# Weights converted into the tiles that TensorE reads, and sums of two batches on VectorE, in a fused attention and mixer kernel

## The chip, the cores and the metric

The kernel runs on one core of a Trainium2 chip. Five engines take part: TensorE (PE; PEld is its loading of weights), VectorE (DVE), ScalarE (ACT), GpSimd (POOL) and SyncE (SP), which here issues every transfer. The metric is the device time of one execution in microseconds, as the median of several runs.

## The reference, cut to what matters

Attention over 4 batches, 12 heads, 448 tokens and 64 channels a head, with a capped score, then two mixers on the result x (4 x 448 x 768):

```python
s = scale * q @ k.T
s = cap * tanh(s / cap)
attn = exp(s - max) / (sum(exp(s - max)) + 1e-9);  x = attn @ v

theta = x @ w_theta                          # 768 x 768
y = w_tok_r @ (x * cos(theta)) + w_tok_i @ (x * sin(theta))   # over tokens
u = x + y;  x = u + relu(u @ w_ch)           # 768 x 768

h = relu(x.T @ w_tok1) @ w_tok2              # 448 -> 256 -> 448, over tokens
u = x + h.T
out = u + relu(u @ w_ch1) @ w_ch2            # 768 -> 1536 -> 768
```

q, k and v come as 32-bit floats, the weights of the mixers as 64-bit floats. The kernel therefore has to turn every weight from a 64-bit word into two 32-bit halves, a high part rounded to the format that TensorE multiplies fast (f32r), and the low rest.

## The kernel before

**Batches.** Attention runs over all four batches, two heads (a head pair) at a time, in four steps of keys for each pair: 24 pairs, 96 steps. The mixers run over two batches at a time: first pair (batches 0 and 1), then second pair (2 and 3). In the first pair the token part (theta and the products over tokens) is done for batch 0 and batch 1 apart, woven into the remaining attention; the second pair follows with no attention left.

**Products.** Every mixer product is three passes, high x high, high x low, low x high (`mm3`), each pass a 128x128 weight tile against 128x448. `gemm(ui, i, ps)` does 18 such passes for one unit of 128 output channels. A unit is a `w` tile of two halves of 768 columns. 36 units make the stream: 0 to 5 w_theta, 6 to 11 w_ch, then four of w_ch1 and four of w_ch2 in turn, three times. `stream` reads w_theta twice in the first pair (batch 0, batch 1), so it has 6 + 36 + 36 places.

**Conversion.** `conv` takes the next piece of the list `conv_list` (half a unit, 128x384, or a part of a token weight): `fetch` loads the 64-bit words into a `raw` tile, and `convert` makes the value with two scalings (`cw` and `raw`; which engine is in `CV` by phase), a shift and an or on VectorE, an add on GpSimd, and then the high half by a cast and the low half by a difference. Before, both halves are written into a small tile `ch`, stored into a cache in HBM (`cu` for units, `ct` for the token weights), and `unit` or `tokmix_gen` loads them again into `w` or `WT`, in the first pair as in the second. One unit is loaded ahead (`AHEAD` = 1); three `w` tiles exist.

**Attention step.** `scores` has TensorE write scores into a bank (`sp`), ScalarE take tanh and exp into a tile `t` (`tm` for the short first step). `av` multiplies with v three steps later (`LAG`). The exponentials' sums come partly from TensorE (products with ones) and partly by adding tiles `t` to one another first: `SUMS` says on which engine, for batches 0 and 1, and 2 and 3 ('p' GpSimd, 'v' VectorE, 'n' none). `finish` copies product and sums out (`EVC`: 'a' ScalarE, 'v' VectorE), sends the sums through HBM to make their inverse (`pk`, `sr`) and broadcast it back (`dn`), and multiplies (`xr` or `XT` with `dn`). The result is split into the halves `XHL`; batches 2 and 3 are put aside in HBM (`xd`) and fetched again (`xl`).

**Token part.** `theta(m)` makes one unit of theta, reduces it to a fraction of a turn on VectorE (`rc`) and takes two sines on ScalarE, which needs another function table than tanh and exp. `zt` transposes the products (`tp`) and splits them into `zn`, `mix` multiplies with the token weights (`tm<-WT,zn` in the trace, a name shared with the short attention tile). `SEQ` gives the order of these steps (t theta, z transposes, x mix, u split, w token weights).

**Order.** Everything is first recorded with a priority by its place in the program. A planner then sets the order on every engine: an engine takes the ready operation of lowest number, and buffers of a ring (`SB`, `PS`) go out in the order in which the program asks for them. `weave` mixes two streams by a ratio (`RATIO`), `every` lets a number of conversions run after each attention step (`PAT`, `PAT1`, `PAT2`), `pri` shifts priorities. Lines of all operations are one helper's line in the trace (L397), so that tiles are read by name.

Of the kernel before, what the change touches and what calls it, by code (L numbers as in the profile page):

```python
# [14 lines left out]
F32R = mybir.dt.float32r  # L15
# [5 lines left out]
B, H, S, D = 4, 12, 448, 64  # L21
DM = H * D
# [13 lines left out]
TWOPI = 6.283185  # L36
HALFPI = float(math.pi / 2)
CW = 384
EVC = 'av'
LAG = 3  # L40
AHEAD = 1
SB = {'kq': 2, 'vt': 2, 'hl': 1, 't': 3, 'tm': 2, 'sv': 2, 'dn': 1, 'xr': 2, 'pk': 3, 'rq': 2, 'w': 3, 'raw': 3, 'cw': 2, 'ch': 2, 'wg': 4, 'zx': 5, 'rc': 4}
PS = {'pa': 2, 'pm': 4}
SUMS = ('pn', 'pp')
CV = ('vvav', 'aavv', 'aaav')
QK = ('vp', 'vp')
XSP = ('v', 'p', 'v')
ZM = ("vv", "pp")
SEQ = ('t0 t1 t2 t3 w z0 x0 t4 z1 x1 t5 u01 z2 x2 z3 x3 u23 z4 x4 u4 z5 x5 u5', 't0 w t1 z0 x0 t2 z1 x1 t3 z2 x2 t4 z3 x3 t5 z4 x4 u01234 z5 x5 u5')
SEQR = "w00 w01 w10 w11 w20 w21 T00 w30 w31 T01 n00 w40 w41 T10 n01 w50 w51 s00 s01 T11 n10 T20 n11 s10 s11 T21 n20 n21 s20 s21"  # L50
CORD = ((0, 0), (1, 0), (0, 1), (2, 0), (1, 1), (3, 0), (2, 1), (3, 1))
CLOSE = 1
ACCM = 2
QREC = 'v'
NATIVE = 2
# [3 lines left out]
PUSH = 15.0  # L59
FIRST = 38  # L60
SECOND = 24
RATIO = ((55, 80.0), (400.0, 130.0))
PAT = (1, 0)
PAT1 = (1, 0, 0)
PAT2 = (1, 0, 0, 0)


def regroup(shape, pattern, sizes):
# [344 lines left out]
def attn_mix_kernel(ctx: ExitStack, tc: tile.TileContext, kqd, vd, cap, wu, wtok, wt1, wt2, out):  # L413
# [5 lines left out]
    pp = ctx.enter_context(tc.tile_pool(name="pp", bufs=1, space=bass.MemoryType.PSUM))  # L419

    plan = Plan(nc)
    plan.tags = {**SB, **PS}
    pe, act, dve, pool, sp_ = (Engine(plan, e) for e in ("PE", "ACT", "DVE", "POOL", "SP"))
    uid = [0]

    def sbuf(name, tag, free, dt=F32, **k):
        uid[0] += 1
        n = f"{name}_{uid[0]}"
        return plan.buf(lambda: sb.tile([P, *free], dt, name=n, tag=tag, bufs=SB[tag]), tag, free, **k)

# [4 lines left out]
    def dram(name, rows, free, whole=False):  # L435
        ap = pd.tile([rows, *free], F32, name=name)
        b = plan.buf(lambda: ap, None if whole else "dram", free, parts=rows, cells=(lambda x: x * 0) if whole else None)
        return b
# [24 lines left out]
    @contextmanager  # L463
    def pri(off):
        plan.off += off
        yield
        plan.off -= off

    def f(v):
        return v.bitcast(F32)  # L470
# [4 lines left out]
    def hi(dst, src):  # L475
        act.copy(dst, src)
# [7 lines left out]
    def times(e, dst, src, by):  # L484
        if e == "a":
            act.mul(dst, src, by)
        else:
            dve.tensor_scalar(out=dst, in0=src, scalar1=by, scalar2=None, op0=ALU.mult)
# [20 lines left out]
    with pri(30):  # L509
# [7 lines left out]
        for j in range(2):  # L517
            at = pick[:, j:j + 1]
# [21 lines left out]
    def fetch(key, src, rows, n):  # L540
        raw = sbuf("raw", "raw", [CW, 2], U32, cells=lambda x: x % 2)[:rows, :n]
        sp_.dma_start(raw.rearrange("p n two -> p (n two)"), src.bitcast(U32))
        return key, raw, rows, n

    def convert(key, raw, rows, n):
        lw, hw = raw[:, :, 0], raw[:, :, 1]
        scale, low, high, rest_ = CV[phase[0]]
        wv = sbuf("cw", "cw", [CW], U32)[:rows, :n]
        times(scale, f(wv), f(hw), 2.0**-112)
        times(low, lw, lw, 2.0**-29)  # L550
        dve.tensor_scalar(out=wv, in0=wv, scalar1=3, scalar2=None, op0=ALU.logical_shift_left)
        dve.scalar_tensor_tensor(out=wv, in0=hw, scalar=0x80000000, in1=wv, op0=ALU.bitwise_and, op1=ALU.bitwise_or)
        pool.tensor_tensor(out=wv, in0=wv, in1=lw, op=ALU.add)
        wv = f(wv)
        hl = sbuf("ch", "ch", [2, CW], F32R)[:rows, :, :n]
        if high == "a":
            hi(hl[:, 0], wv)
        else:
            dve.tensor_copy(out=hl[:, 0], in_=wv)
        (lo_pool if rest_ == "p" else lo)(hl[:, 1], wv, hl[:, 0])  # L560
        name, i, j = key
        if (name, i) not in cache:
            cols = {"u": DM, "t": S, "a": 4 * DT, "b": 2 * S}[name]
            cache[name, i] = dram(f"c{name}{i}", rows, [2, cols])
        sp_.dma_start(cache[name, i][:, :, j * n:(j + 1) * n], f(hl))
# [26 lines left out]
    fetched = []  # L592
    done = set()

    def conv(n=1):
        for _ in range(n):
            while len(fetched) < 3:
                p = next(pieces, None)
                if p is None:
                    break  # L600
                with pri(-60):
                    fetched.append(fetch(*p))
            if fetched:
                x = fetched.pop(0)
                convert(*x)
                done.add(x[0])

    def weight(name, i, dst, parts):
        while any((name, i, j) not in done for j in range(parts)):
            conv()  # L610
        if dst is not None:
            sp_.dma_start(f(dst), cache[name, i])

    WT = {}
    WS = {}

    def tokmix_gen(pr):
        for i in range(4):
            n = min(2, NT7 - 2 * i)
            t = sbuf("WT", "wg", [2, 2 * S], F32R)  # L620
            for j in range(n):
                weight("t", 2 * i + j, t[:, :, j * S:(j + 1) * S], 2)
                WT[2 * i + j] = t[:, :, j * S:(j + 1) * S]
                yield

    def load_tok(pr):
        w1 = [sbuf("W1", "rc", [1024], F32R)[:CP] for h in range(2)]
        w2 = [sbuf("W2", "rc", [1024], F32R)[:, :2 * S] for h in range(2)]
        for name, w, parts in (("a", w1, NK), ("b", w2, 4)):
            weight(name, 0, None, parts)  # L630
            for h in range(2):
                sp_.dma_start(f(w[h]), cache[name, 0][:, h])
        WS[1] = [w.rearrange("p (c o) -> p c o", o=DT) for w in w1]
        WS[2] = [w.rearrange("p (c o) -> p c o", o=S) for w in w2]

    stream = order[:6] + order + order
    units = {}

    def unit(i):
        for j in range(i, min(i + AHEAD + 1, len(stream))):  # L640
            if j not in units:
                t = sbuf("w", "w", [2, DM], F32R)
                with pri(-100):
                    weight("u", stream[j], t, DM // CW)
                units[j] = t
        return units[i]
# [5 lines left out]
    def attn(batches):  # L652
# [45 lines left out]
        def av(b, hp, c):  # L698
            vt, hl, kq, acc, pt = st[b, hp]
            mode = SUMS[b // 2]  # L700
            if c == 0:
                if b < ACCM:
                    acc = [psum("av"), None]
# [60 lines left out]
        def finish(b, hp, acc):  # L764
            if b < CLOSE:
                return close(b, hp, acc)
# [39 lines left out]

    EV = EVC

    def split(dst, src):
# [4 lines left out]
        hi(h, src)  # L814
        (lo_pool if XSP[phase[0]] == "p" else lo)(l, src, h)

# [14 lines left out]
    def token(pr, which):  # L831
# [64 lines left out]

        for op in SEQ[pr].split():
            k, m = op[0], op[1:]
# [25 lines left out]
    def rest(pr):  # L924
# [12 lines left out]
        def tok1(t, i):  # L937
            W1 = WS[1]
            xn = [sbuf("xn", "zx", [1024], F32R)[:CP] for h in range(2)]
# [21 lines left out]
        def tok2(t, i):  # L961
            h1, W2 = h1s[t, i], WS[2]
            for j in range(2):
# [73 lines left out]
    def run(gen):  # L1037
        for _ in gen:
            pass
# [6 lines left out]
    ga = attn(range(B))  # L1046
    run(every(steps(ga, FIRST), PAT))
    phase[0] = 1
    weave(token(0, (0,)), every(steps(ga, SECOND), PAT1), *RATIO[0])
    weave(chain(token(0, (1,)), rest(0)), every(ga, PAT2), *RATIO[1])  # L1050
    late[0] = True
# [46 lines left out]
```

## Time and profile before

| | |
|---|---|
| median of 3 runs | 975.23 us (974.08 to 976.71) |
| profiled execution | 978.4 us, its span 976.6 us |
| granted TensorE clock, mean | 0.993 |
| TensorE, VectorE, ScalarE, GpSimd busy | 956.8, 540.5, 413.6, 270.8 us |
| moved by transfers | 173.62 MB, mean 178 GB/s |

The span goes from the first to the last instruction; what the profiled execution takes beyond it lies before and behind. Times in the trace are counted from the start of the span. Matmuls are pipelined: the time of one (367 ns for 448 columns) is its passage, and what counts for the sum is the distance from start to start. An entry in brackets behind an instruction is the idle time of its engine ahead of it, and who ended it. The granted clock is a share of the full 2.4 GHz.

### The profile page before, as it was taken

Reading aid. Unit: us, or ns where it says so; the run is one execution under the profiler, and the core shown is the slowest. Engines: PE = TensorE matmul, PEld = TensorE weight load, DVE = VectorE, ACT = ScalarE, POOL = GpSimd, SP = SyncE. Lnnn points to the kernel's source line nnn. Section 1 sums busy time; section 2 is a strip of 40 time slices with the busy share of each in tenths; the row PEclk is TensorE's granted clock in tenths of the full one; section 3 lists DMA queues with packets and bytes.
Section 4 is the critical chain, followed back from the end, with each engine's and each line's share of the span. In section 5 each row is a group of like instructions: output and inputs, shape, how many; then the busy total and the mean of one; then the engine's idle time right before and its main releaser. Section 6 shows DMA issues by size and latency. Waiting matters only on the chain.

```text
span 976.6 us, 13210 instructions
## 1 busy us (share of the span) xinstructions
PE 956.8 (98%) x4938; PEld 733.5 (75%) x4938; DVE 540.5 (55%) x927; ACT 413.6 (42%) x645; POOL 270.8 (28%) x208
## 2 busy tenths in 40 slices
PE   9999999999999999999999999999999999999998
PEld 2223445476778886877877799899999889999997
DVE  7776577779876679774656672243623441212222
ACT  7788887748762546433443340333401221010010
POOL 3544234654532455441422340313200000000000
PEclk9999989999999999999999999999999999999999
DMA  7866867558567665796686678611311203223233
GB/s 246 272 199 190 259 199 240 164 166 280 184 182 254 214 218 186 234 313 209 209 271 205 217 249 301 253 37 61 108 65 65 65 1 130 97 97 130 81 132 127
DMA packets 76488, 173.62 MB, mean 178 GB/s; under 512 B 9864, under 2 KB 52744, under 8 KB 76424
## 3 DMA queue, kind: packets, MB, share of 16 engines
q1 hardware_dynamic: 76424, 172.78, 54.3%
q8 instruction: 39, 0.64, 0.3%
q14 instruction: 25, 0.20, 0.1%
HBM read 130.94 MB, written 41.68 MB: 177 GB/s over the span
## 4 chain that ended last, share of the span: by engine, by line
PE 84%; DVE 6%; DMA 5%; ACT 3%; issue 2%; POOL 0%; SPq 0%; ACTq 0%; DVEq 0%; POOLq 0%
PE c L397 36%; PE wc L397 9%; PE av L397 7%; PE tm L397 7%; PE th L397 7%; PE sp L397 7%; PE t L397 5%; DMA dn<-sr 4%; PE sm L397 3%; PE xp L397 2%; DVE rc L397 2%; DVE ch L397 1%; PE tp L397 1%; ACT t L397 1%; DVE cw L397 1%
## 5 line engine op out<-in xcount | busy, mean ns | idle before, releaser
L397 PE MATMUL c<-g,w 128*128 128x448 f32 x864 | 179.1, 367 | 0.0
L397 PE MATMUL c<-XHL,w 128*128 128x448 f32 x846 | 175.8, 367 | 0.6 <-POOL XHL L397 0.6
L397 PEld LDWEIGHTS c<-g,w 128*128 128x128 f32 x864 | 161.7, 188 | 19.4 <-issue 4.3
L397 PEld LDWEIGHTS c<-XHL,w 128*128 128x128 f32 x846 | 158.3, 188 | 19.3 <-issue 2.9
L397 POOL TENSOR_TENSOR cw<-cw,raw 128x384 uint32<-128x384 uint32 (+2 forms) x94 | 91.7, 977 | 238.7 <-DVE cw L397 121.8
L397 PE MATMUL tm<-WT,zn 128*128 128x448 f32 x483 | 113.5, 383 | 5.0 <-DVE zn L397 3.1
L397 PEld LDWEIGHTS tm<-WT,zn 128*128 128x128 f32 x483 | 90.7, 194 | 23.6 <-DVE zn L397 6.5
L397 DVE TENSOR_TENSOR XT<-c,XT 128x448 f32<-128x448 f32 x72 | 44.9, 624 | 103.4 <-PE c L397 103.4
L397 ACT ACTIVATE g<-c 128x448 fp32r<-128x448 f32 x47 | 25.6, 544 | 164.5 <-PE c L397 164.4
L397 PE MATMUL th<-XHL,w 128*128 128x448 f32 x432 | 94.2, 369 | 0.0
L397 POOL TENSOR_TENSOR t<-t,t 128x896 f32<-128x896 f32 x36 | 80.7, 2241 | 40.2 <-PE av L397 25.0
L397 ACT ACTIVATE t<-sp,consts 128x896 f32<-128x896 f32 x72 | 72.1, 1004 | 46.3 <-PE av L397 26.6
L397 PEld LDWEIGHTS th<-XHL,w 128*128 128x128 f32 x432 | 79.9, 188 | 13.3 <-issue 5.5
L397 PE MATMUL wc<-XHL,w 128*128 128x448 f32 x414 | 86.9, 367 | 0.0
L397 PEld LDWEIGHTS wc<-XHL,w 128*128 128x128 f32 x414 | 77.3, 188 | 7.9 <-DVE XT L397 1.4
L397 DVE TENSOR_TENSOR ch<-cw,ch 128x384 fp32r<-128x384 f32 (+2 forms) x94 | 73.1, 777 | 12.0 <-ACT ch L397 9.7
L397 DVE SCALAR_TENSOR_TENSOR g<-c,g 128x448 fp32r<-128x448 f32 x47 | 29.3, 623 | 88.8 <-ACT g L397 88.7
L397 ACT ACTIVATE t<-t,consts 128x896 f32<-128x896 f32 x72 | 75.0, 1043 | 2.0
L397 ACT ACTIVATE cw<-raw 128x384 f32<-128x384 f32 (+2 forms) x75 | 38.8, 520 | 84.4 <-DVE ch L397 74.1
L397 PE MATMUL av<-t,vt 128*64 128x448 f32 x288 | 66.5, 559 | 0.0
L397 PE MATMUL sp<-kq 64*128 64x448 f32 (+1 forms) x240 | 60.8, 590 | 3.0 <-ACT t L397 3.0
L397 DVE SCALAR_TENSOR_TENSOR cw<-raw,cw 128x384 uint32<-128x384 uint32 (+2 forms) x94 | 56.9, 605 | 2.6
(128 smaller groups left out, 1113.5 us busy)
## 6 DMA issues: line engine op xcount, KB each, us to landing
w<-cu SPq DMA_DIRECT2D x78, 768.0 KB
raw<-wu SPq DMA_DIRECT2D x72, 384.0 KB
cu<-ch SPq DMA_DIRECT2D x72, 384.0 KB
kq<-kqd SPq DMA_DIRECT2D x24, 448.0 KB
WT<-ct SPq DMA_DIRECT2D x14, 448.0 KB
vt<-vd SPq DMA_DIRECT2D x24, 224.0 KB
out<-XT SPq DMA_DIRECT2D x24, 224.0 KB
dn<-sr SPq DMA_DIRECT2D x18, 224.0 KB
```

What stands on the lines that cost most here:

```text
L397: getattr(eng[o.eng], name)(*map(real, a), **{x: real(y) for x, y in k.items()})
```

## The change

Weights of the first pair are converted into the tile that TensorE reads. `home` gives that place: a `w` tile for a unit, the `WT` tile for a token weight; the tile `ch` is gone, and what has no such place takes a `w` tile too. From the cache are loaded only the units of w_theta and w_ch in the first pair, and everything in the second pair. The 24 units of w_ch1 and w_ch2 (`direct`) are not converted after attention steps but when `unit` asks for them, one ahead (`FRESH`); the store into the cache stays, from the `w` tile. Loads are two units ahead instead of one where they remain. Two raw pieces are fetched ahead instead of three.

With it go: the sums of batches 2 and 3 on VectorE instead of GpSimd (`SUMS`), the copies of batches 0 and 1 in `finish` and `close` on VectorE instead of ScalarE (`EVC`), the cast of the high half on ScalarE in the second phase (`CV`), the low halves of `usplit` in the first pair on VectorE (`XSP`), four tiles `t` instead of three, a ring `zx` of four instead of five, another order of the token part of the first pair (`SEQ`), and other ratios and patterns of weaving.

```diff
@@ -36,20 +36,24 @@
 TWOPI = 6.283185
 HALFPI = float(math.pi / 2)
 CW = 384
-EVC = 'av'
+EVC = 'vv'
 LAG = 3
-AHEAD = 1
-SB = {'kq': 2, 'vt': 2, 'hl': 1, 't': 3, 'tm': 2, 'sv': 2, 'dn': 1, 'xr': 2, 'pk': 3, 'rq': 2, 'w': 3, 'raw': 3, 'cw': 2, 'ch': 2, 'wg': 4, 'zx': 5, 'rc': 4}
+AHEAD = 2
+SB = {'kq': 2, 'vt': 2, 'hl': 1, 't': 4, 'tm': 2, 'sv': 2, 'dn': 1, 'xr': 2, 'pk': 3, 'rq': 2, 'w': 3, 'raw': 3, 'cw': 2, 'wg': 4, 'zx': 4, 'rc': 4}
 PS = {'pa': 2, 'pm': 4}
-SUMS = ('pn', 'pp')
-CV = ('vvav', 'aavv', 'aaav')
+SUMS = ('pn', 'vv')
+CV = ('vvav', 'aaav', 'aaav')
 QK = ('vp', 'vp')
-XSP = ('v', 'p', 'v')
+XSP = ('v', 'v', 'v')
 ZM = ("vv", "pp")
-SEQ = ('t0 t1 t2 t3 w z0 x0 t4 z1 x1 t5 u01 z2 x2 z3 x3 u23 z4 x4 u4 z5 x5 u5', 't0 w t1 z0 x0 t2 z1 x1 t3 z2 x2 t4 z3 x3 t5 z4 x4 u01234 z5 x5 u5')
+SEQ = ('t0 t1 t2 w z0 x0 t3 z1 x1 t4 z2 x2 t5 u012 z3 x3 u3 z4 x4 u4 z5 x5 u5', 't0 w t1 z0 x0 t2 z1 x1 t3 z2 x2 t4 z3 x3 t5 z4 x4 u01234 z5 x5 u5')
 SEQR = "w00 w01 w10 w11 w20 w21 T00 w30 w31 T01 n00 w40 w41 T10 n01 w50 w51 s00 s01 T11 n10 T20 n11 s10 s11 T21 n20 n21 s20 s21"
 CORD = ((0, 0), (1, 0), (0, 1), (2, 0), (1, 1), (3, 0), (2, 1), (3, 1))
 CLOSE = 1
+DIR = 12
+FRESH = 1
+RAWS = 2
+CVP = 0
 ACCM = 2
 QREC = 'v'
 NATIVE = 2
@@ -59,10 +63,10 @@
 PUSH = 15.0
 FIRST = 38
 SECOND = 24
-RATIO = ((55, 80.0), (400.0, 130.0))
-PAT = (1, 0)
+RATIO = ((55, 35.0), (400.0, 240.0))
+PAT = (1, 1, 0, 1, 0)
 PAT1 = (1, 0, 0)
-PAT2 = (1, 0, 0, 0)
+PAT2 = (1, 1, 0, 1, 0)
 
 
 def regroup(shape, pattern, sizes):
@@ -542,6 +546,21 @@
         sp_.dma_start(raw.rearrange("p n two -> p (n two)"), src.bitcast(U32))
         return key, raw, rows, n
 
+    open_ = {}
+
+    def home(key, rows, n):
+        name, i, j = key
+        if name == "u":
+            if i not in open_:
+                open_[i] = sbuf("w", "w", [2, DM], F32R)
+            return open_[i][:, :, j * n:(j + 1) * n]
+        if name == "t":
+            if i // 2 not in WT0:
+                WT0[i // 2] = sbuf("WT", "wg", [2, 2 * S], F32R)
+            at = (i % 2) * S + j * n
+            return WT0[i // 2][:, :, at:at + n]
+        return sbuf("ch", "w", [2, DM], F32R)[:rows, :, :n]
+
     def convert(key, raw, rows, n):
         lw, hw = raw[:, :, 0], raw[:, :, 1]
         scale, low, high, rest_ = CV[phase[0]]
@@ -552,7 +571,7 @@
         dve.scalar_tensor_tensor(out=wv, in0=hw, scalar=0x80000000, in1=wv, op0=ALU.bitwise_and, op1=ALU.bitwise_or)
         pool.tensor_tensor(out=wv, in0=wv, in1=lw, op=ALU.add)
         wv = f(wv)
-        hl = sbuf("ch", "ch", [2, CW], F32R)[:rows, :, :n]
+        hl = home(key, rows, n)
         if high == "a":
             hi(hl[:, 0], wv)
         else:
@@ -592,34 +611,41 @@
     fetched = []
     done = set()
 
-    def conv(n=1):
+    def direct(key):
+        return key[0] == "u" and key[1] >= DIR
+
+    def conv(n=1, force=False):
         for _ in range(n):
-            while len(fetched) < 3:
+            while len(fetched) < RAWS:
                 p = next(pieces, None)
                 if p is None:
                     break
                 with pri(-60):
                     fetched.append(fetch(*p))
-            if fetched:
+            if fetched and (force or not direct(fetched[0][0])):
                 x = fetched.pop(0)
-                convert(*x)
+                with pri(CVP if force else 0):
+                    convert(*x)
                 done.add(x[0])
 
     def weight(name, i, dst, parts):
         while any((name, i, j) not in done for j in range(parts)):
-            conv()
+            conv(force=True)
         if dst is not None:
             sp_.dma_start(f(dst), cache[name, i])
 
     WT = {}
     WS = {}
+    WT0 = {}
 
     def tokmix_gen(pr):
         for i in range(4):
             n = min(2, NT7 - 2 * i)
-            t = sbuf("WT", "wg", [2, 2 * S], F32R)
+            if pr:
+                t = sbuf("WT", "wg", [2, 2 * S], F32R)
             for j in range(n):
-                weight("t", 2 * i + j, t[:, :, j * S:(j + 1) * S], 2)
+                weight("t", 2 * i + j, t[:, :, j * S:(j + 1) * S] if pr else None, 2)
+                t = t if pr else WT0[i]
                 WT[2 * i + j] = t[:, :, j * S:(j + 1) * S]
                 yield
 
@@ -637,8 +663,12 @@
     units = {}
 
     def unit(i):
-        for j in range(i, min(i + AHEAD + 1, len(stream))):
+        for j in range(i, min(i + (FRESH if 6 + DIR <= i < 42 else AHEAD) + 1, len(stream))):
             if j not in units:
+                if 6 + DIR <= j < 42:
+                    weight("u", stream[j], None, DM // CW)
+                    units[j] = open_[stream[j]]
+                    continue
                 t = sbuf("w", "w", [2, DM], F32R)
                 with pri(-100):
                     weight("u", stream[j], t, DM // CW)
```

ScalarE's order in the token part of the first pair; `rc` are the sines, `t` a tanh of scores `sp`, `zn` the split of transposes, `cw` and `raw` conversions. Before, at the pair of tables that the trace has at 129.25 and 134.35 us, two thetas share it:

```order
L397 ACT_TABLE_LOAD
L397 ACTIVATE rc_1204<-rc_1204,consts 128x448
L397 ACTIVATE rc_1204<-rc_1204 128x448
L397 ACTIVATE rc_1132<-rc_1132,consts 128x448
L397 ACTIVATE rc_1132<-rc_1132 128x448
L397 COPY XT<-av_1126 128x448
L397 COPY sv_1257<-sm_1227 128x448
L397 CAST zn_1266<-tp_1244 128x512
L397 ACTIVATE raw_1098<-raw_1098 128x224
L397 ACT_TABLE_LOAD
L397 ACTIVATE t_1275<-sp_1201,consts 128x896
```

Now, at the second such pair:

```order
L401 ACT_TABLE_LOAD
L401 ACTIVATE rc_1053<-rc_1053,consts 128x448
L401 ACTIVATE rc_1053<-rc_1053 128x448
L401 CAST WT_1024<-cw_1071 128x224
L401 ACTIVATE raw_1010<-raw_1010 128x224
L401 CAST zn_1112<-tp_1095 128x512
L401 ACTIVATE cw_1118<-raw_1010 128x224
L401 CAST WT_1024<-cw_1037 128x224
L401 ACT_TABLE_LOAD
L401 ACTIVATE t_1126<-sp_1105,consts 128x896
```

One theta stands between two tables where two stood, the copies out of attention are gone, and casts into `WT` stand there instead. Counting table loads on ScalarE from the first theta product to the first w_ch product gives 16 before and 24 now. Conversions there are fewer: 12 instead of 18 large ones have both scalings on ScalarE. Attention steps are 38 instead of 35 by TensorE's order, 39 instead of 35 by the tanh on ScalarE, that is up to four more.

VectorE's order in the channel products of the first pair; `c` are products in PSUM, `XT` the sum they are added to, `xr` and `sv` copies out of attention. Before:

```order
L397 CAST ch_4208<-cw_4095 128x384
L397 TENSOR_TENSOR ch_4208<-cw_4095,ch_4208 128x384
L397 TENSOR_TENSOR XT<-c_704_4195,XT 128x448
L397 TENSOR_SCALAR cw_4222<-cw_4222 128x384
L397 SCALAR_TENSOR_TENSOR cw_4222<-raw_4060,cw_4222 128x384
L397 COPY xr_4236<-av_3953 128x448
L397 CAST ch_4241<-cw_4151 128x384
L397 COPY sv_4250<-av_3953 128x448
L397 TENSOR_TENSOR ch_4241<-cw_4151,ch_4241 128x384
```

Now, in the same products:

```order
L401 TENSOR_TENSOR w_4117<-cw_4086,w_4117 128x384
L401 TENSOR_TENSOR XT<-c_689_4098,XT 128x448
L401 TENSOR_SCALAR cw_4134<-cw_4134 128x384
L401 SCALAR_TENSOR_TENSOR cw_4134<-raw_4069,cw_4134 128x384
L401 TENSOR_TENSOR w_4117<-cw_4107,w_4117 128x384
L401 TENSOR_TENSOR XT<-c_695_4124,XT 128x448
L401 TENSOR_TENSOR XT<-c_696_4150,XT 128x448
```

The differences go into `w` itself, the casts have left for ScalarE, and attention has ended before. The second half of `w_4117` stands behind the addition of product 689; its first use on TensorE comes more than two products of 18 passes later.

## Rows read from the trace of the kernel before

**Rows 1.** The page: busy us, share of the span, instructions of each engine.
```profile
PE 956.8 (98%) x4938; PEld 733.5 (75%) x4938; DVE 540.5 (55%) x927; ACT 413.6 (42%) x645; POOL 270.8 (28%) x208
```
**Rows 2.** Stretches: length, busy (instructions) of each engine, clock, DMA share, GB/s.
```profile
0.00:92.60 92.60, 90.48 (x451) 24.58 (x451) 69.55 (x143) 75.51 (x100) 41.97 (x38) 1.00 0.72 229
92.60:290.00 197.40, 186.50 (x941) 118.74 (x940) 148.54 (x258) 147.14 (x227) 88.72 (x67) 0.97 0.68 210
290.00:402.00 112.00, 111.53 (x642) 88.85 (x640) 83.32 (x138) 53.24 (x84) 48.33 (x33) 1.00 0.69 218
402.00:606.00 204.00, 203.69 (x1013) 166.95 (x1014) 125.33 (x215) 72.00 (x120) 63.90 (x49) 1.00 0.73 243
606.00:811.00 205.00, 202.58 (x1105) 185.62 (x1104) 78.11 (x118) 54.28 (x94) 27.87 (x24) 1.00 0.26 89
811.00:976.60 165.60, 161.97 (x794) 148.78 (x793) 35.61 (x57) 11.46 (x21) 0.00 (x0) 1.00 0.33 113
```
**Rows 3.** The chain that ended last: start, us, what; its longest piece.
```profile
811.40 161.58 PE c L397 x792
```
**Rows 4.** TensorE in order of time, token stretch: start, us, instruction, idle before.
```profile
136.71 1.76 PE L397 MATMUL sp<-kq 64*64 64x448 f32 x4 [2.31 <-ACT t L397]
...
172.31 0.97 PE L397 MATMUL av<-tm,vt 64*64 64x448 f32 x4 [2.17 <-ACT t L397]
...
212.21 2.45 PE L397 MATMUL tm<-WT,zn 128*128 128x448 f32 x9 [1.11 <-ACT zn L397]
...
279.60 5.66 PE L397 MATMUL tm<-WT,zn 128*128 128x448 f32 x19 [2.11 <-DVE zn L397]
```
**Rows 5.** ScalarE in order of time, ahead of the first of these waits.
```profile
134.35 1.28 ACT L397 ACT_TABLE_LOAD   x1
135.65 1.91 ACT L397 ACTIVATE t<-sp,consts 128x896 f32<-128x896 f32 x2
```
**Rows 6.** VectorE in order of time, ahead of the last of these waits.
```profile
276.13 0.63 DVE L397 TENSOR_TENSOR xr<-xr,dn 128x448 f32<-128x448 f32 x1 [2.65 <-DMA dn<-sr]
...
278.87 1.14 DVE L397 TENSOR_TENSOR zn<-tp,zn 128x512 fp32r<-128x512 f32 x2
```
**Rows 7.** Windows of ten microseconds, columns as in rows 2; the clock is third last.
```profile
130.00:140.00 10.00, 7.69 (x38) 2.67 (x31) 6.62 (x14) 9.97 (x17) 3.09 (x3) 0.81 0.81 262
140.00:150.00 10.00, 10.00 (x49) 6.18 (x50) 6.40 (x13) 6.37 (x12) 3.19 (x4) 0.85 0.52 157
170.00:180.00 10.00, 7.83 (x31) 3.33 (x32) 3.77 (x10) 5.92 (x8) 2.83 (x2) 0.83 0.62 187
...
280.00:290.00 10.00, 10.00 (x52) 8.01 (x52) 7.65 (x17) 6.77 (x11) 4.89 (x5) 0.85 0.92 280
```
**Rows 8.** Groups on ScalarE, 92.6 to 290: busy us, mean ns, idle before, releasers.
```profile
L397 ACT ACTIVATE t<-t,consts 128x896 f32<-128x896 f32 x28 | 29.1, 1043 | 0.7
...
L397 ACT ACT_TABLE_LOAD x16 | 20.5, 1283 | 0.2
...
L397 ACT ACTIVATE cw<-raw 128x384 f32<-128x384 f32 x12 | 6.6, 550 | 12.3 <-DVE ch L397 6.9 <-DMA raw<-wu 3.6 <-POOL t L397 1.8
...
L397 ACT COPY XT<-av 128x448 f32<-128x448 f32 x4 | 2.1, 522 | 2.4 <-PE av L397 2.4
```
**Rows 9.** Transfers, 92.6 to 290.
```profile
DMA packets 22456, 41.46 MB, mean 210 GB/s; under 512 B 3469, under 2 KB 17160, under 8 KB 22440
```
**Rows 10.** Groups by shape: on GpSimd (92.6 to 290), on VectorE (whole span).
```profile
L397 POOL TENSOR_TENSOR t<-t,t 128x896 f32<-128x896 f32 x14 | 31.2, 2228 | 22.3 <-PE av L397 12.7 <-ACT t L397 9.2
...
L397 DVE TENSOR_TENSOR ch<-cw,ch 128x384 fp32r<-128x384 f32 x72 | 59.6, 827 | 5.4 <-ACT ch L397 3.7 <-issue 0.2
...
L397 DVE TENSOR_TENSOR XHL<-XT,XHL 128x896 fp32r<-128x896 f32 x12 | 14.0, 1172 | 7.1 <-ACT XHL L397 6.9
```
**Rows 11.** GpSimd and VectorE in order of time, one beside the other.
```profile
155.62 4.97 POOL L397 TENSOR_TENSOR t<-t,t 128x896 f32<-128x896 f32 x2
...
155.81 2.06 DVE L397 SCALAR_TENSOR_TENSOR pk<-pk,consts 56x16 f32<-56x16 f32 x1
```

## The prediction

> **What bounds the kernel now.** I read the busy times first, then the stretches, then the waits inside the one stretch that loses time. TensorE is busy 98% of the span, VectorE 55%, ScalarE 42%, GpSimd 28% [rows 1]; what the change can win is time in which TensorE idles or runs at its lower clock. The table of stretches [rows 2] finds it. Attention alone (0 to 92.6) has 2.1 us of idle TensorE, of which 1.4 is the start. The token stretch, from the first theta product to the first product with w_ch of the first pair (92.6 to 290), has 197.40 - 186.50 = 10.9 us, and a mean granted clock of 0.97, which by 3% of 197.4 is another 5.9: together 16.8. The next two have 0.5 and 0.3, the second pair 2.4 (606 to 811), the rest 3.6, nearly all of it the last stores. In the dense end 792 products take 161.58 us, 204 ns each [rows 3], and nothing hides there. So about 20 us of 976.6 can be had at all, and 16.8 of them lie in the token stretch.
>
> There two kinds of wait make the long gaps. **ScalarE's function tables:** at 136.71 the scores product waits 2.31 for the activation that empties its bank, at 172.31 the product with v waits 2.17 [rows 4]. Ahead of the first ScalarE loaded a table at 134.35 for 1.28 and began the tanh at 135.65 [rows 5]: it had changed to sine and back. **VectorE held by a transfer:** at 276.13 it had idled 2.65 for the normaliser's row (dn<-sr), and the split of the transposed z, queued behind, started at 278.87 [rows 6]; TensorE waited 2.11 at 279.60, and 1.11 at 212.21 in the same way [rows 4]. After each gap of over 2 us the granted clock is 0.81 to 0.85 for ten microseconds [rows 7], that is part of the time at 1.2 instead of 2.4 GHz. A window of ten at 0.85 costs up to 1.5: the three gaps cost 1.9 + 1.5 after the first, 1.7 with the second, 1.5 after the third. So tables cost 2.31 + 2.17 + 5.1 = 9.6, the held VectorE 2.11 + 1.11 + 1.5 = 4.7, and 16.8 - 9.6 - 4.7 = 2.5 are short waits.
>
> **The change, part by part**, against the profiled execution (978.4 us, 1.8 of it outside the span, and 3.2 above the median of 975.2).
>
> *Table switches.* By the order, ScalarE loads a table 24 times instead of 16 in the token stretch: every theta is now on its own, with scores between. At 1283 ns [rows 8] that is +10.3 us of ScalarE. The two copies that stood between sine and tanh (522 ns each, rows 8) go to VectorE, 8 in the stretch, -4.2. Casts of the high halves come over from VectorE, net 12 large and 9 small; but fewer pieces are converted here, and ScalarE scales 12 large and 10 small operands less. A large scaling takes 550 ns [rows 8], and a cast of that size is priced alike, so these cancel. Without attention ScalarE gets +6.1 on top of 147.1 [rows 2]. The stretch also takes in four more attention steps, three of 128x896 and one of half that, each a tanh and an exp (1043 ns for a large exp in [rows 8], the tanh taken alike): 3.5 x 2 x 1.043 = +7.3 on ScalarE, and on TensorE about 9.8 (90.48 busy over the 37 steps ahead of the first theta, rows 2), which leaves the later stretches. What do the waits become? At the old price, 9.6 over 8 switches there and back, 12 cost 14.4: +4.8. Against that, the 1.0 us of copies goes out of the very wait of 2.31, and a fourth tile for the exponentials lets ScalarE be one step further ahead, some 2.1 us, about the length of a long wait: if that covers all, -9.6. I take half the old price, 12 x 0.6 = 7.2, so -2.4 (from -9.6 to +4.8), since the row of the first wait shows nearly half of it to be the copies.
>
> The Trainium skill (ScalarE: Activation LUTs, What ACT_TABLE_LOAD costs) speaks against this part: it gives a switch as the load of 1283 ns and a drain of about 1380 behind it, 2.66 us. The trace has the load at that length, but the tanh starts 0.02 us after it ends [rows 5]. By the page's figure the eight more loads would be 21.3 us of ScalarE, by the rows 10.3.
>
> *The normaliser's transfer.* 41.46 MB pass in the token stretch [rows 9]. The tiles for the token product are now written by the conversion itself, so seven loads of 448 KB, 3.2 MB, go, and some six conversions' raw words and stores, about 3 MB: 15% less in the queue. The wait for dn stays where it was in VectorE's order, a transfer behind a shorter queue. I take 2.0 of the 4.7 off (0 to 4.7).
>
> *Sums of batches 2 and 3.* Twelve sums of 128x896 leave GpSimd in this stretch (2228 ns each) for VectorE; no row has them there, and the nearest, a difference of the same size, is 1172 ns [rows 10]: +14 us of VectorE. But beside two such sums on GpSimd a 56x16 instruction of VectorE took 2.06 us [rows 11], and that goes too; so do 26 casts of VectorE, while 11 low halves come to it from GpSimd. VectorE stands at 148.5 of 197.4. I put the balance at -0.5 (-2 to +2, the short waits gone or doubled).
>
> *Direct weights of the channel products* (24 units, 48 pieces, in 402 to 606 of the kernel before). Their 24 loads of 768 KB go, but TensorE was busy 203.69 of 204 [rows 2]: nobody waited for them, so 0. What hides the conversions is their lead: in VectorE's order the second half of a tile is written two or more products of 18 x 204 ns before its first use. If that cover is gone, each unit shows its last difference, 0.83 us [rows 10].
>
> *The small ring zx, 5 to 4.* It holds the split z, xn and h. One split less can wait ready; where these matter in the second pair TensorE idles 2.4 now [rows 2]. +0.4 (0 to +2.4).
>
> *Attention out of the channel stretch* (its last step now ends before the channel products): the same work, at full clock before and after, 0.
>
> Sum: -2.4 - 2.0 - 0.5 + 0.4 = -4.5, so 973.9 for an execution like the profiled one, and **970.7** against the median.
>
> **Rivals.** (1) *ScalarE sets the token stretch, slower.* It has 147.1 of 197.4 us now and is the releaser of the two table waits; it gets 6.1 + 7.3 = 13.4 more. If the stretch goes on at 197.4 / 147.1 = 1.34 us for each of ScalarE's, it grows by 18.0, and 9.8 of that is TensorE's work brought forward: +8.2, 983.4. It decides from where the fourth tile no longer bridges a switch. For it: the 12 switches; against it: between 290 and 402 ScalarE is at half, with TensorE never waiting. (2) *No net change:* gaps closed at one switch open at the next, 975 within 2. For it: TensorE has no slack elsewhere, and loads and queue time saved in the channel stretch are worth nothing. (3) *All long gaps go,* and with them the slow clock: -9.6 - 4.7, 960.9. For it: three gaps make most of the loss and each has its cause touched; against it: eight more table loads. (4) *Late weights:* the 24 units each wait 0.83: +19.9, 995. Against it is the lead of two products.
>
> **How the numbers follow.** Forecast 0.40 (its own range 966 to 974), rival 3 0.14, rival 2 0.18, rival 1 0.23, rival 4 0.05. About 0.3%, 2.9 us, is what a measurement can tell from no change: faster is under 972.3, slower over 978.1. The forecast lies on the faster side with 0.36 of its 0.40; with rival 3 faster is 0.50. Same is 0.04 + 0.18 = 0.22, slower 0.28. The range runs from 958 (rival 3 and some of the short waits) to 986 (rival 1 and the ring), with rival 4 outside and a little of each end.
>
> **What would show it.** Right: in the new token stretch the idle of TensorE is 6 to 8 us, with at most two gaps over 2 us and a clock of 0.98; 24 table loads on ScalarE there; VectorE's waits for dn are shorter than 2.65; the channel stretch stays full; the second pair takes its 370 us. Wrong: TensorE waits on ScalarE's tanh or exp at most switches (rival 1), VectorE above 90% there with z late (then the sums were mis-sized), waits for w in the channel stretch (rival 4), or a clock of 1.00 throughout (rival 3).

## The result, and the profile after

| | before | after |
|---|---|---|
| median (range) | 974.72 (974.08 to 976.71) | 964.64 (964.50 to 965.35) |
| profiled execution, its span | 978.4, 976.6 | 964.5, 962.7 |
| granted TensorE clock, mean | 0.993 | 1.000 |
| moved by transfers | 173.62 MB | 151.53 MB |

The ratio is 0.9895 (0.9878 to 0.9912): 10.1 us faster, where 4.5 were forecast. 964.64 lies inside the range given, between the forecast and rival 3. The profiled execution of before was 3.7 us above its median and that of after at its median, so the rows below differ by 13.9 where the medians differ by 10.1.

The page of the kernel after, engines busy, answers [rows 1]; then its stretches, cut at the same events as [rows 2] (columns as there):

```profile
PE 949.1 (99%) x4938; PEld 731.2 (76%) x4938; DVE 532.3 (55%) x920; ACT 444.4 (46%) x702; POOL 188.4 (20%) x166
```
```profile
0.00:93.90 93.90, 91.03 (x454) 24.89 (x455) 81.69 (x160) 73.50 (x94) 44.13 (x39) 1.00 0.73 236
93.90:286.00 192.10, 187.45 (x986) 118.00 (x985) 144.92 (x259) 163.30 (x239) 48.38 (x41) 1.00 0.58 181
286.00:417.00 131.00, 130.83 (x756) 95.15 (x758) 79.94 (x134) 67.63 (x103) 18.09 (x17) 1.00 0.50 151
417.00:592.00 175.00, 175.00 (x858) 159.56 (x851) 112.43 (x195) 74.28 (x154) 49.97 (x46) 1.00 0.70 219
592.00:797.00 205.00, 202.70 (x1104) 185.30 (x1103) 77.68 (x118) 54.26 (x95) 27.86 (x24) 1.00 0.25 87
797.00:962.70 165.70, 162.11 (x792) 148.31 (x790) 35.61 (x57) 11.42 (x21) 0.00 (x0) 1.00 0.33 112
```

The difference lies in the second row. The token stretch idles 192.10 - 187.45 = 4.65 us at a clock of 1.00, where 10.9 and some 5.9 of slow clock were lost: 12.2 of the 16.8 are back. The channel stretch idles nowhere (175.00 of 175.00), the second pair takes 370.7 against 370.6, and the dense end has the same pace, 792 products in 162.20 us, as [rows 3]:

```profile
796.92 162.20 PE c L401 x792
```

TensorE in order of time, all that is left of waits in the token stretch, against [rows 4]:

```profile
224.63 0.97 PE L401 MATMUL sp<-kq 64*64 64x448 f32 x4 [1.94 <-DVE xr L401]
240.78 0.88 PE L401 MATMUL sp<-hl 64*128 64x448 f32 x6 [0.95 <-ACT tm L401]
...
282.91 0.68 PE L401 MATMUL tm<-WT,zn 128*128 128x448 f32 x2 [1.22 <-ACT zn L401]
284.12 2.10 PE L401 MATMUL tm<-WT,zn 128*128 128x448 f32 x9 [0.53 <-DVE zn L401]
```

No wait on ScalarE's `t` of over half a microsecond remains there (the 0.95 for the short tile `tm` has no table load ahead of it), though the groups on ScalarE in this stretch have 24 table loads for 16 [rows 8]:

```profile
L401 ACT ACTIVATE t<-t,consts 128x896 f32<-128x896 f32 x30 | 31.3, 1043 | 0.7
L401 ACT ACT_TABLE_LOAD x24 | 30.8, 1283 | 0.4
```

One switch there and back, ScalarE in order of time against [rows 5], and what TensorE does meanwhile:

```profile
133.24 1.28 ACT L401 ACT_TABLE_LOAD   x1
134.54 0.67 ACT L401 ACTIVATE rc<-rc,consts 128x448 f32<-128x448 f32 x1
135.11 0.56 ACT L401 ACTIVATE rc<-rc 128x448 f32<-128x448 f32 x1
135.58 0.36 ACT L401 CAST WT<-cw 128x224 fp32r<-128x224 f32 x1
135.96 1.28 ACT L401 ACT_TABLE_LOAD   x1
137.26 1.01 ACT L401 ACTIVATE t<-sp,consts 128x896 f32<-128x896 f32 x1
```
```profile
133.26 3.95 PE L401 MATMUL tm<-WT,zn 128*128 128x448 f32 x18
```

The switch takes ScalarE 4.0 us (133.24 to 137.26), against 6.4 at the place shown before (129.25 to 135.65), where two thetas shared it. Just then TensorE has 18 token products, which need no tanh. A short switch alone does not hide itself: the one ahead of the second wait of [rows 4] (2.17 at 172.31) took 4.2, with one theta and no copy out of attention in it:

```profile
167.06 1.28 ACT L397 ACT_TABLE_LOAD   x1
...
171.25 1.01 ACT L397 ACTIVATE t<-sp,consts 128x896 f32<-128x896 f32 x1
```

VectorE's waits for `dn` are longer than in [rows 6], not shorter, though fewer bytes pass than in [rows 9]. Then the totals of such waits for the products `xr<-xr,dn` over the whole span, before and after (total, times, longest):

```profile
223.40 0.62 DVE L401 TENSOR_TENSOR xr<-xr,dn 128x448 f32<-128x448 f32 x1 [4.35 <-DMA dn<-sr]
...
279.78 0.63 DVE L401 TENSOR_TENSOR xr<-xr,dn 128x448 f32<-128x448 f32 x1 [3.80 <-DMA dn<-sr]
```
```profile
DMA packets 18748, 34.69 MB, mean 181 GB/s; under 512 B 3429, under 2 KB 14061, under 8 KB 18733
```
```profile
DVE xr L397 <- DMA dn<-sr: 16.1, 10, 2.9
DVE xr L401 <- DMA dn<-sr: 34.8, 11, 4.3
```

The sums, which no row of before had on VectorE, take 1097 ns there, half of GpSimd's 2228 [rows 10]; and `pk`, the 56x16 instruction of [rows 11], takes 386 ns in the mean, against 823 before (last line):

```profile
L401 DVE TENSOR_TENSOR t<-t,t 128x896 f32<-128x896 f32 x24 | 26.3, 1097 | 2.9 <-PE av L401 2.3
...
L401 DVE SCALAR_TENSOR_TENSOR pk<-pk,consts 56x16 f32<-56x16 f32 x18 | 7.0, 386 | 1.5 <-DMA pk<-sv 1.5
L397 DVE SCALAR_TENSOR_TENSOR pk<-pk,consts 56x16 f32<-56x16 f32 x18 | 14.8, 823 | 1.4 <-DMA pk<-sv 1.4
```

### The profile page after: what moved, and what is told of

It is laid out like the page before. It is cut to its first block, busy times and chain, and to the rows that moved or that the text cites. A ratio compares the mean times of both kernels' runs of the same rounds, so it can differ in the third digit from the quotient of the medians.

```text
span 962.7 us, 13126 instructions
## 1 busy us (share of the span) xinstructions
PE 949.1 (99%) x4938; PEld 731.2 (76%) x4938; DVE 532.3 (55%) x920; ACT 444.4 (46%) x702; POOL 188.4 (20%) x166
## 2 busy tenths in 40 slices
DMA packets 71128, 151.53 MB, mean 157 GB/s; under 512 B 9368, under 2 KB 50456, under 8 KB 71064
## 4 chain that ended last, share of the span: by engine, by line
PE 91%; DVE 5%; DMA 2%; ACT 2%; issue 1%; POOL 0%; SPq 0%; DVEq 0%; ACTq 0%
PE c L401 36%; PE tm L401 10%; PE wc L401 9%; PE th L401 9%; PE av L401 7%; PE t L401 6%; PE sp L401 6%; PE sm L401 2%; PE tp L401 2%; DMA dn<-sr 2%; PE xp L401 2%; DVE cw L401 1%; ACT t L401 1%; DVE raw L401 1%; DVE w L401 1%
## 5 line engine op out<-in xcount | busy, mean ns | idle before, releaser
L401 PEld LDWEIGHTS c<-g,w 128*128 128x128 f32 x864 | 162.3, 188 | 13.9
L401 PE MATMUL tm<-WT,zn 128*128 128x448 f32 x483 | 107.6, 372 | 2.3 <-ACT zn L401 1.8
L401 PEld LDWEIGHTS tm<-WT,zn 128*128 128x128 f32 x483 | 88.3, 188 | 17.6 <-issue 3.5
L401 PE MATMUL th<-XHL,w 128*128 128x448 f32 x432 | 96.4, 372 | 0.0
L401 DVE SCALAR_TENSOR_TENSOR cw<-raw,cw 128x384 uint32<-128x384 uint32 (+2 forms) x94 | 64.3, 685 | 2.7
L401 ACT CAST w<-cw 128x384 fp32r<-128x384 f32 x72 | 35.1, 508 | 45.2 <-POOL cw L401 16.5
L401 DVE TENSOR_TENSOR w<-cw,w 128x384 fp32r<-128x384 f32 x72 | 48.8, 693 | 7.2 <-ACT w L401 7.1
L401 PEld LDWEIGHTS av<-t,vt 128*64 128x64 f32 x288 | 15.8, 135 | 38.9 <-issue 35.7
```

What stands on the lines that cost most here:

```text
L401: getattr(eng[o.eng], name)(*map(real, a), **{x: real(y) for x, y in k.items()})
```

## The experiments

"In its own order" means that the planned order of every engine stays, and only the edit is made when it is written out. The kernel before was timed beside each group again (medians 973.6 to 974.5); differences are against these, or against 964.64 for the kernel after, which was not timed again. The fences show what an edit comes to, in short.

**1 and 2: the sums alone.** The sums of batches 2 and 3 are issued on the other engine, in each kernel's own order.

```diff
-  dve.tensor_tensor(out=pt[1], in0=pt[1], in1=pt[c], op=ALU.add)    # after, batches 2, 3
+  pool.tensor_tensor(out=pt[1], in0=pt[1], in1=pt[c], op=ALU.add)   # 1; the reverse in before: 2
```


> The changed kernel with its 24 sums of batches 2 and 3 back on GpSimd, every engine's order otherwise as it is (the sums keep their place in the common order). Theory A (the sums on GpSimd held VectorE, and that made the long gaps): back up by 5 to 10 us, 970 to 975, with gaps over 2 us and a lower clock in the token stretch. Theory B (the order of the token part removed them): 0 to 2 us, 964.6 to 967, clock 1.00.

> The kernel before with the same 24 sums on VectorE, the order otherwise as it is. Theory A: 5 to 10 us faster, 965 to 970. Theory B: 973 to 976, the waits at the two table switches unchanged (2.31 and 2.17 us).

Measured: 969.01 (967.70 to 969.73), 4.4 slower than after, between the bands of the two theories; and 967.23 (965.50 to 967.78), ratio 0.9928 (0.9913 to 0.9943), 6.9 faster than before, in theory A's band. In the first TensorE waits twice, 0.7 us each, for a sum itself. In the second the mean `pk` falls from 823 to 422 ns, and TensorE's waits for `zn` fall from 4.7 us (3.1 for VectorE's half, 1.6 for ScalarE's) to 1.5 (0.2 and 1.3); both table waits stay:

```profile
137.14 0.97 PE L397 MATMUL sp<-kq 64*64 64x448 f32 x4 [2.31 <-ACT t L397]
...
169.88 0.97 PE L397 MATMUL av<-tm,vt 64*64 64x448 f32 x4 [1.63 <-ACT t L397]
```

VectorE took on 24 sums, 27.1 us, and was busy no longer for it: 537.3 us in all, against 540.5 [rows 1]. Its other instructions became close to 30 us shorter. `pk` is 7.2 of that; the cast `ch<-cw` of 128x384, which has one input, falls from 581 to 478 ns. VectorE's waits for `dn`, those of `XT` and `xr` together, mostly stay (18.3 us over the span, against 20.9).

```profile
PE 950.5 (98%) x4938; PEld 731.3 (76%) x4938; DVE 537.3 (56%) x951; ACT 414.4 (43%) x645; POOL 219.3 (23%) x184
```
```profile
L397 DVE TENSOR_TENSOR t<-t,t 128x896 f32<-128x896 f32 x24 | 27.1, 1131 | 6.2 <-PE av L397 6.0
```

**3 and 4: each half of the change alone**, planned anew.

```diff
 3: after's code, with EVC, SUMS, CV, XSP, SEQ, RATIO, PAT, PAT2 and the rings t, zx of before
 4: before's code (everything through the cache), with those of after
```


> The direct weights alone: the changed code with the engines, rings t and zx, sequence and weaving of before (the order is planned anew). Theory C (fewer transfers and no way through the cache make the gain): 965 to 969, waits for the normaliser's row shorter. Theory B: 973 to 977, long gaps at table switches still there.

> The other half alone: the kernel before, weights through the cache, with the engines, rings t and zx, sequence and weaving of after (planned anew). Theory B: 965 to 969, clock 0.998 or more. Theory C: 973 to 977.

Measured: 983.30 (982.99 to 985.20) and 995.86 (994.47 to 997.46). Both are slower than before, outside the bands of both theories. Waits of TensorE, summed by pair (total, times, longest): in the third (first line) the largest is for VectorE's half of `zn`; in the fourth they begin with the token weights, which the earlier token products now want from the cache:

```profile
PE tm L401 <- DVE zn L401: 7.5, 5, 3.9
...
PE tm L397 <- DMA WT<-ct: 14.2, 3, 8.0
PE sp L397 <- ACT t L397: 7.3, 4, 4.2
```

**5: sums that nobody reads.** After, in its own order; behind each sum on VectorE GpSimd gets one of the same size over a tile of its own.

```diff
   dve.tensor_tensor(out=pt[1], in0=pt[1], in1=pt[c], op=ALU.add)
+  pool.tensor_tensor(out=junk, in0=junk, in1=junk, op=ALU.add)       # 128x896
```


> The kernel after, in its own order, with the sums of batches 2 and 3 left on VectorE; behind each, GpSimd gets one sum of 128x896 over a tile of its own that nobody reads (24 of them). Theory A (a sum on GpSimd is dear because it holds VectorE, whoever reads it): most of the +4.4 us of the first experiment comes back, 967 to 970, and VectorE's small pk instruction takes 0.44 us or more in the mean against 0.39. Theory D (the sum itself is late for the product that reads it, 2.2 us on GpSimd against 1.1 on VectorE): nobody waits for these, so 964 to 965.5.

Measured: 975.94 (974.26 to 978.36), 11.3 slower than after, above the bands of both theories. Nobody reads these sums, so sums on GpSimd have a price without being late for a reader. Its size is not that of the first experiment: here VectorE keeps its own 24 sums, and these now take 1568 ns instead of 1097, 11.3 us more in all; another part can be GpSimd's own later work, queued behind. My sign for it was wrong: `pk` stays at 383 ns, but others are held. Two `rc<-rc,XT` that take 1.15 us together in after, ahead of the same `pk` (first line), take 3.90, as long as GpSimd's two sums beside them:

```profile
217.49 1.15 DVE L401 TENSOR_TENSOR rc<-rc,XT 128x448 f32<-128x448 f32 x2
```
```profile
220.20 3.70 POOL L405 TENSOR_TENSOR junk<-junk 128x896 f32<-128x896 f32 x2
```
```profile
220.49 3.90 DVE L402 TENSOR_TENSOR rc<-rc,XT 128x448 f32<-128x448 f32 x2
```
```profile
L402 DVE TENSOR_TENSOR t<-t,t 128x896 f32<-128x896 f32 x24 | 37.6, 1568 | 2.9 <-PE av L402 2.3
```

The Trainium skill (SBUF — State Buffer, Who interferes with whom) has the rule: a VectorE instruction with both inputs in SBUF and a GpSimd instruction that reads SBUF exclude each other for a whole instruction. The rows of 3.70 and 3.90 us agree with it.

**6, 7 and 8: no table switches.** In their own orders the sines are issued as tanh. This leaves out the sines and all table loads but one (18 before, 26 after, over the whole span).

```diff
-  act.activation(rc, rc, AF.Sin)
+  act.activation(rc, rc, AF.Tanh)      # 6: before; 7: before with the edit of 2; 8: after
```


> The kernel before, in its own order, with the sines taken as tanh, so that ScalarE loads no second table (18 loads become 1; left out: the sines). Theory B (the prediction's term: the switches cost 2.31 + 2.17 us of gaps and 5.1 of clock behind them): 975 - 9.6 = 965 to 967. Theory E (the gap opens again behind the next late one, VectorE held by GpSimd): 971 to 974.

> The kernel before, in its own order, with the 24 sums on VectorE as in the second experiment (967.2) and the sines taken as tanh (left out: the sines). Theory B: the two table waits left in that run (2.31 and 1.63 us, and some 2 of clock) go as well: 961 to 963, under the kernel after. Theory E: 966 to 967, the waits come from something else.

> The kernel after, in its own order, with the sines taken as tanh (26 table loads become 1; left out: the sines). Theory B: the fourth tile of exponentials and the copies taken off ScalarE already hide the switches, so 964 to 965. Rival 1 of the prediction (ScalarE sets the token stretch): 25 loads of 1.28 us are 32 us of ScalarE, and a part of these shows: 955 to 961.

Measured: 966.36 (966.13 to 966.44), 7.6 less than before; 962.05 (961.65 to 962.99), 11.9 less than before and 5.2 less than the second; 965.32 (964.07 to 967.93), no less than after. Switches cost before 7.6 us, near the 9.6 of the prediction, and cost after nothing that can be seen: rival 1 falls. Sums and switches overlap (6.9 + 7.6 against 11.9). Without switches the old order with the sums moved (962.05) is 3.3 faster than the kernel after (965.32). Nothing here shows that the rest of the change pays, beyond the sums, in any other way than by hiding switches.

**9: the fourth with direct token weights only.**

```diff
-  weight("t", 2*i + j, t[:, :, j*S:(j+1)*S], 2)                                # loads from the cache
+  weight("t", 2*i + j, t[:, :, j*S:(j+1)*S] if pr else None, 2); t = t if pr else WT0[i]
```


> The fourth experiment (all that is not direct weights: engines, rings, token order, ratios; 995.9) with one thing more: the token weights of the first pair are converted straight into the WT tiles. The weights of the channel products still go through the cache. Theory F (the earlier token order fails on its own because TensorE waits 6.0 and 8.0 us for WT from the cache): both waits and the slow clock behind them go, 975 to 983. Theory C (the direct tiles of the 24 channel units matter as well): 985 to 993.

Measured: 989.06 (988.20 to 989.96), 6.8 less than the fourth, in theory C's band and slower than theory F's. The waits for `WT<-ct` are gone. Others have come (6.7 for `zn`, 5.3 for `t`), so that this new plan says little on the channel units.

**10 and 11: no wait for the normaliser.** In their own orders the product takes a constant tile; the division is left out.

```diff
-  dve.tensor_tensor(out=x, in0=x, in1=dn, op=ALU.mult)
+  dve.tensor_tensor(out=x, in0=x, in1=flat, op=ALU.mult)      # 10: after; 11: before
```


> The kernel after, in its own order; the 24 products with dn take a constant tile in its place, so that VectorE waits no more for the normaliser's transfer (left out: the division by the sums). Theory G (VectorE held by dn is what is left in the token stretch, 1.94 + 1.22 + 0.53 us behind waits of up to 4.35): 960.5 to 962. Theory H (what follows on VectorE is late in any case): 964 to 965.

> The kernel before, in its own order, with the same edit (left out: the division by the sums). Theory G with the prediction's size (2.11 + 1.11 of gaps and 1.5 of clock): 4.7 less than 974, so 969 to 970. Theory H: 972.5 to 974.5.

Measured: 961.69 (961.31 to 963.03), 3.0 less than after; 972.05 (969.57 to 972.67), 2.0 less than before, ratio 0.9980 (0.9964 to 0.9996), nearer to theory H's band than to G's. The wait for `dn` cost before less than half of the 4.7 that I gave it. In the tenth the first wait of the token stretch stays (1.85 us, where 1.94 stood): VectorE's copy into `xr` now waits for the store of an older `xr`. So two tiles `xr` held that place as well as `dn` did.

```profile
223.94 0.62 DVE L404 COPY xr<-av 128x448 f32<-128x448 f32 x1 [4.44 <-DMA xd<-xr]
```

**12: all sums on VectorE**, after, in its own order; the 12 of batches 0 and 1 as well.

```diff
-SUMS = ('pn', 'vv')
+SUMS = ('vn', 'vv')     # by the edit of 2, without a new plan
```


> The kernel after, in its own order, with the 12 sums of batches 0 and 1 on VectorE too: a version that could beat both. Theory A (each sum on GpSimd holds VectorE): 24 of them are worth 4.4 us, but these 12 stand in the first 92 us where TensorE idles 2.9 us in all, 1.4 of that at the start, so 963 to 964.4. Theory I (VectorE is the fuller engine there, and 1.1 us each on it are late for TensorE): 965.5 to 968.

Measured: 964.96 (963.35 to 968.50), between the two theories. No gain can be seen, as theory A's reason has it: in the first 92 us TensorE has little to win.

**13 and 18: only drawn anew.** One planner constant is changed.

```diff
-PUSH = 15.0
+PUSH = 12.0     # 13: after; 18: before
```


> The kernel after with one constant of the planner's search changed (how far a late operation is hurried, 15 to 12), nothing else: the same work in an order drawn anew. Theory J (the order itself is luck): 969 to 980, as far off as the third experiment. Theory C (the edits decide, not the drawing): 963 to 967.

> The kernel before with the one constant of the planner's search changed (15 to 12). Theory C (the drawing matters little): 972 to 977. Theory J (the order is luck, and 9 to 21 us of the halves' losses may be that): under 968 or over 981.

Measured: 962.14 (961.55 to 962.36) and 969.28 (968.49 to 970.73): -2.5 and -4.3, outside the ranges of theory C and of theory J alike. A neutral drawing moves either kernel by some microseconds, less than theory J asked. The losses of 3, 4 and 9 (+9.2, +21.8, +15.0) are beyond that, but two drawings are no distribution. Between these two, which were not timed together, the change is worth 7.1 by the medians; over the four pairings of drawings it is worth 4.6 (969.28 to 964.64) to 12.6 (974.72 to 962.14).

**14 and 15: parts of the cover of the switches**, after, planned anew.

```diff
-'t': 4          +'t': 3            # 14
-EVC = 'vv'      +EVC = 'av'        # 15
```


> The kernel after with three tiles t instead of four. Theory K (the prediction's: the fourth tile lets ScalarE run one step ahead and bridges a switch): waits of over 1 us for t behind the table loads come back, 967 to 972. Theory L (it is the copies' move or the order of the thetas): within 2 us of the kernel after drawn anew.

> The kernel after with the copies of batches 0 and 1 out of attention on ScalarE again. Theory M (the 1 us of copies between sine and tanh made nearly half of each table wait): 967 to 971, with waits for t of 1 to 2 us behind the loads. Theory K: within 2 us of the kernel after drawn anew.

Measured: 971.20 (969.30 to 972.96) and 967.24 (966.03 to 968.40), 9.1 and 5.1 slower than the thirteenth, 6.6 and 2.6 slower than after. Both lie in the band of their theory, yet the trace of the fourteenth has one long wait for `t`, behind a load that was itself late, and its longest wait, 4.05 us, comes from `dn`, for which VectorE stood ahead of the copy `sv` (last line):

```profile
174.76 0.57 ACT L401 CAST XHL<-XT 128x448 fp32r<-128x448 f32 x1 [4.92 <-DVE XT L401]
175.35 1.28 ACT L401 ACT_TABLE_LOAD   x1
```
```profile
177.70 1.18 PE L401 MATMUL av<-tm,vt 64*64 64x448 f32 x4 [2.17 <-ACT t L401]
...
259.62 0.68 PE L401 MATMUL sp<-hl 64*128 64x448 f32 x4 [4.05 <-DVE sv L401]
```
```profile
258.41 0.63 DVE L401 TENSOR_TENSOR xr<-xr,dn 128x448 f32<-128x448 f32 x1 [4.27 <-DMA dn<-sr]
```

The fifteenth has 1.35 and 1.02 for `t` again, and its longest, 2.48, for `xr` of VectorE. Taking away either part alone costs between 2.6 and 9.1 by these references, and with drawings worth 2.5 to 4.3 their shares can't be told apart.

**16 and 17: the product with dn later.** After, in its own order but for this: the 12 products `xr<-xr,dn` stand seven instructions later on VectorE, their stores behind them. 17 adds a third tile `xr` and a second `dn`.

```diff
-order = self.plan()
+order = later(self.plan(), 7)      # xr<-xr,dn and its store, behind 7 more of VectorE
-bufs=SB[tag]
+bufs=SB[tag] + (tag in ("xr", "dn"))   # 17 only, with the order of 16
```


> The kernel after, in its own order but for one thing: the 12 products xr<-xr,dn of batches 2 and 3 stand seven instructions later on VectorE, and their stores later on the queue. Theory G (VectorE stands still for up to 4.35 us while dn travels): seven instructions of some 0.62 us cover that, 962 to 963, what the tenth experiment gained but with nothing left out. Theory H (what is moved ahead of it is no earlier for TensorE): 964 to 965.5.

> The sixteenth experiment (981.3) with three xr tiles instead of two and two dn instead of one, in the same order on every engine. Theory N (the loss was the copy into xr that waits for the store of the tile before the last, 9.6 us at 228.84): the long waits go, and with G's cover 961.5 to 963.5. Theory H (moving the products is of no use): 964 to 967 without those waits.

Measured: 981.27 (980.75 to 982.47), and with the tiles 959.07 (958.23 to 960.11), ratio 0.9848 (0.9827 to 0.9870): the first above, the second below the bands of its theories. The seventeenth is the fastest version that computes everything, 5.6 under after, more than the 3.0 of the tenth. Three tiles `xr` without the later order were not tried, so the shares of order and tiles stay open. In the sixteenth three waits of TensorE (7.0, 3.5 and 5.8 us) make the loss; each stands behind a copy into `xr`. VectorE in order of time, ahead of the first: the copy waits for a store that leaves later now:

```profile
219.04 0.25 DVE L401 RECIPROCAL pk<-pk 56x16 f32<-56x16 f32 x1
228.84 0.62 DVE L401 COPY xr<-av 128x448 f32<-128x448 f32 x1 [9.55 <-DMA xd<-xr]
```

The seventeenth at the same place, and its token stretch, in which TensorE is busy throughout:

```profile
218.13 0.62 DVE L401 TENSOR_TENSOR xr<-xr,dn 128x448 f32<-128x448 f32 x1
...
219.63 0.55 DVE L401 COPY xr<-av 128x448 f32<-128x448 f32 x1
```
```profile
93.90:281.00 187.10, 187.10 (x986) 118.00 (x985) 145.24 (x260) 163.78 (x241) 48.63 (x42) 1.00 0.60 185
```

## Why the prediction was too small

**Sums of batches 2 and 3: the step that failed.** "I put the balance at -0.5 (-2 to +2, the short waits gone or doubled)." Measured, they are worth -6.9 alone and -4.4 inside after. The row that told it was there: 2.06 us for 56x16 elements [rows 11], against a least time of 217 ns in the same trace. I priced that as one instruction instead of asking how much of VectorE's work stands beside the 24 sums that move: VectorE got close to 30 us back, more than the 27.1 that it took on. The waits for `zn`, which I had given to `dn`, fell from 4.7 to 1.5 with the sums, without any other edit (second experiment). `pk` also starts the transfer `dn`, but that is not the main way: VectorE's waits for `dn` hardly fell there, and the kernel before gained only 2.0 when it waited for no `dn` at all, where the sums gave 6.9.

**Table switches: mis-sized too.** The old price was right (9.6, measured 7.6), and so was the place. "I take half the old price" was not: the new kernel hides all 24 loads of the stretch, and on top of the moved sums that is worth up to 5.2 (967.23 to 962.05), where 2.4 were forecast. ScalarE became fuller, by 16.2 where 13.4 were forecast (163.3 of 192.1), and sets nothing; the large scalings that I counted off it did not leave (`cw<-raw` of 128x384 stands 12 times in the stretch after, as in [rows 8]). The copies were not nearly half of the old price either: the second old wait had none ahead of it. That TensorE has token products during a switch is seen at one place (133.26); which of tile, copies and order does most stays open, and the old token order in after was not tried.

**The normaliser's transfer.** -2.0 forecast; no gain is to be seen. All of it was worth 2.0 before (0.4 to 3.5 by the interval) and is worth 3.0 after, so the change may have cost about 1. Fewer bytes did not shorten the wait (4.35 where [rows 6] had 2.65). Whether VectorE only comes to the product earlier, or the transfer itself takes longer, no run here separates.

**The rest.** Channel weights 0, attention out of the channel stretch 0: right, the stretch is full. The ring zx +0.4: nothing seen. Rival 4 did not come. By the signs given, rival 3 came nearest: no gap over 2 us (1.94 the longest), 4.65 us of idle where the forecast had 6 to 8, a clock of 1.00; it had the waits behind `dn` gone as well, and a part of these stayed.

**The sum by what was measured:** -6.9 (sums) - 5.2 (switches on top of them) + 1.0 (dn) = -11.1, against -10.1. The pieces come from different orders, and a drawing moves 2.5 to 4.3, so the agreement to 1 is better than the method. For the same reason a part of the miss is luck of the drawing: the least of the four pairings, 4.6, would have met the forecast of 4.5, with the terms as wrong as they are. Moving the sums alone gives 6.9 of the 10.1; all the rest of the change gives 2.6 (967.23 to 964.64), which is within a drawing. The direct weights earn little in transfers; what is shown is that the new token order without direct token weights waits 14.2 us for them. Whether the channel units must be direct as well is not shown.

## What to carry to other kernels

Before pricing a move between GpSimd and VectorE, look in the trace for small VectorE instructions that take many times their least time, and price everything that stands beside GpSimd's long ones: here VectorE took on 27.1 us of sums and was busy no longer. A wait in an in-order queue can be moved behind later work, but count the buffers that the moved instruction keeps: the same order lost 16.6 us with two tiles `xr` and one `dn`, and gained 5.6 with three and two. Where a planner draws the order, measure a neutral drawing before a difference of a few microseconds is given to an edit.

## What was not expected of the hardware

Twenty-four sums on GpSimd that nobody reads cost a kernel with TensorE 99% busy 11.3 us. They hold two-input VectorE instructions, for up to a whole GpSimd instruction (3.90 us beside 3.70; VectorE's own sums took 1568 ns instead of 1097), and what queues on GpSimd may add to it. One-input casts became longer beside sums on GpSimd too (581 ns in before, 478 in the second experiment). In this kernel a table switch is the load alone: the row before the load at 135.96 ends, and the row behind it starts, within 0.02 us of it, and 25 loads fewer took 32.3 us off ScalarE (444.4 to 412.1), 1.29 each.
